# Attention with two expert layers on one core: the last tile pair closed tile by tile, the first two score tiles as whole float32 products, and 64-token products with both words side by side

## The chip, the cores and the metric

The kernel runs on one core of one Trainium2 chip. The metric is the device time of one execution in microseconds (us). Three runs of the kernel before gave 1182.36, 1183.76 and 1184.87 us; their median is 1183.76 us. Engines are named as in the profile: PE is TensorE's products (PEld its weight loads), DVE is VectorE, ACT is ScalarE, POOL is GpSimd, SP issues the DMAs.

## What is computed

```python
scores = q @ k.T / sqrt(64)                 # 4 batches x 8 heads, 576 x 576
mask   = scores >= (32nd largest of the row)
attn   = exp(where(mask, scores, -1e9) - rowmax)
attn   = attn / (attn.sum(-1) + 1e-9)
x      = attn @ v                           # 2304 tokens x 512
h      = relu(x @ w_in);  x = (h * h) @ w_out            # first expert layer, d_ff = 2048
h      = x @ w_in2;       out = max(0.01*h, h) @ w_out2  # second expert layer
```

All inputs are float32; the expert weights arrive as 64-bit words, of which the kernel builds float32 on the chip.

## The kernel before

**Precision.** A product is made of float32 words split in two: a high word that TensorE multiplies in one pass (type `fp32r`) and the low word that is left. `split_q` and `split_k` make the words of q and k: ACT or POOL copies the high word (`split_hi`, L129 and L131), DVE or POOL subtracts (L289, L272). q and k of a head come stored twice, in partitions 0 to 63 and 64 to 127; k keeps its high word in the first and its low word in the second, so that two products, with q's high and q's low word, give one score half. Products whose operands are typed plain float32 (`av`, L436, and the transposes L350, L365, L386) need no words.

**Attention.** The 2304 tokens are cut into units of 256, 64 or 320 tokens of a batch (`UNITS`). A unit and a pair of heads (`uh`) give tiles of 128 score rows, and two tiles are a pair of 16 slots on a time scale. For each tile `scores` makes two halves of 288 keys in PSUM and ACT copies them to `s` (L310, L311). The 32 largest of each row come from seven DVE instructions: four MAX8 (L932), each of eight values, and three MATCH_REPLACE8 between them (L934). Then `drop` (L329) and `expo_sum` (L333) on ACT make the exponentials, `recip` (L338 to L341) the reciprocal sums, `pt_main` (L350, L360) and `pt_left` (L365 to L401) the transposed probabilities `PT` and the row of reciprocals `rb`, `av` (L436) the product with v, and `x_out` (L467, L468, L472) the normed result and its two words xh and xl, the expert layers' input.

**The two stages.** The first block of the expert layers holds 512 tokens: units 0 and 1, which are pairs 0 to 15. The last of these pairs (`first_done`, 15) closes the block, and the expert layers start then, on PE; the attention of the other units runs on beside them, with probabilities in two words (`norm`, `av_split` L447, L452, L453). Unit 3 has 64 tokens: its `av_split` makes for each head eight products with 64 columns (four chunks of keys, high and low word) and one for the rest.

**Expert layers.** `moe` goes through 16 slices of d_ff. For each it makes h (L653), the activation and its two words ga, gh, gl (L663 to L673), and adds to acc (L690 in layer one, L692 in layer two). The weights of each slice are converted once from the raw words: ACT copies the low (L543) and high part (L552), DVE joins them (L559), ACT and POOL split them (L563, L564). The first two slices' weights are converted ahead, in `lead_passes` (L583, L584) and `lead_bits` (L590, L591, two DVE passes each: the shifted bits, then the sign).

**What sets the order.** The program lists its steps by slot (`at`), `urgent` raises a step's priority, `behind(key)` puts an instruction behind another of its engine. A scheduler then lays down a fixed order for each engine and for each DMA queue, and a pool's buffers can add waits. Each engine works through its order strictly.

## Time and profile before

| | |
|---|---|
| Runs, median (lowest to highest) | 1183.76 us (1182.36 to 1184.87) |
| Profiled execution, its own time | 1181.85 us |
| Its span, first to last instruction | 1180.1 us |
| Around the span | 1.75 us |
| Busy: PE, PEld, DVE, ACT, POOL | 1120.4, 984.7, 840.8, 817.0, 746.4 us |
| Mean granted TensorE clock | 0.989 of full speed |

The span falls in a stage before the expert layers, to 184.45 us, in which attention alone runs, and the rest, in which PE works almost without a break. A share of the whole span therefore says little; each stage has its own limit.

### The profile page before, as it was taken

The page shows a single profiled execution, that of the slowest core. Times are in us where ns is not written, and L with a number is a line of the kernel's source. Part 1 is how long each engine was busy: PE and PEld are TensorE (multiplying, and loading weights), DVE is VectorE, ACT ScalarE, POOL GpSimd, SP SyncE. Part 2 cuts the span into 40 slices and gives each one's busy share as a digit, 9 for nine tenths or more (in the row PEclk, how much of TensorE's full clock was granted, in tenths as well). Part 3 has the DMA queues.
Part 4 walks back from the last instruction along what each step waited for, and adds up shares of the span by engine and source line. Part 5 has one row for each costly group of instructions (what it writes and reads, how often), then busy time and mean ns, then how long its engine had stood idle before and what let it go on. Part 6 is the DMA issues. An engine that isn't in the chain of part 4 may idle for free.

```text
span 1180.1 us, 20025 instructions
## 1 busy us (share of the span) xinstructions
PE 1120.4 (95%) x6376; PEld 984.7 (83%) x6376; DVE 840.8 (71%) x1771; ACT 817.0 (69%) x1823; POOL 746.4 (63%) x960
## 2 busy tenths in 40 slices
PE   5898978899899999999999999999999999999998
PEld 4777766687678899989999998888788899999997
DVE  7999998867675669999999999989999200110011
ACT  6899997999889778877677677556866633333322
POOL 7968837899878767667898776767756543002100
PEclk9899988999999999999999999999999999999999
DMA  9768766999999588899988888667676489779974
GB/s 305 271 211 285 252 223 220 376 344 326 341 339 363 213 325 287 274 308 373 328 284 297 300 273 306 227 209 236 228 229 205 156 319 341 258 249 355 345 256 135
DMA packets 108201, 329.53 MB, mean 279 GB/s; under 512 B 17216, under 2 KB 25408, under 8 KB 104000
## 3 DMA queue, kind: packets, MB, share of 16 engines
q1 hardware_dynamic: 105472, 323.53, 79.3%
q10 hardware_dynamic: 2624, 4.72, 1.1%
q8 instruction: 52, 0.85, 0.3%
q14 instruction: 53, 0.43, 0.1%
HBM read 257.03 MB, written 71.17 MB: 278 GB/s over the span
## 4 chain that ended last, share of the span: by engine, by line
PE 70%; ACT 10%; DVE 7%; DMA 3%; issue 2%; POOL 2%; ACTq 0%; SPq 0%; POOLq 0%; DVEq 0%
PE h L653 28%; PE acc L692 15%; PE acc L690 13%; PE att L447 4%; DVE m L932 4%; PE att L350 3%; DVE w L934 3%; PE att L436 2%; ACT stage L311 1%; ACT e L333 1%; PE att L310 1%; PE sp L310 1%; ACT e L329 1%; ACT s L311 1%; DMA vraw<-in_v_dram 1%
## 5 line engine op out<-in xcount | busy, mean ns | idle before, releaser
L653 PE MATMUL h<-xh,wi 128*128 128x512 f32 (+2 forms) x1280 | 346.4, 343 | 8.8 <-ACT xh L704 3.5
L932 DVE MAX8 m<-w 128x8 f32<-128x576 f32 x432 | 311.1, 747 | 2.2
L653 PEld LDWEIGHTS h<-xh,wi 128*128 128x128 f32 x1280 | 226.1, 189 | 34.9 <-ACT ga L670 4.8
L673 POOL TENSOR_TENSOR gl<-ga,gh 128x512 fp32r<-128x512 f32 (+2 forms) x160 | 162.3, 1017 | 126.6 <-ACT gh L672 108.6
L934 DVE MATCH_REPLACE8 w<-m,w 128x576 f32<-128x576 f32 x288 | 213.0, 742 | 0.6
L653 PE MATMUL h<-xl,wi 128*128 128x512 f32 (+2 forms) x640 | 204.5, 339 | 0.0
L358 POOL TENSOR_TENSOR PTs<-whole,PTs 128x512 fp32r<-128x512 f32 x112 | 144.5, 1297 | 43.3 <-ACT whole L357 39.8
L690 PE MATMUL acc<-gh,wo 128*128 128x512 f32 (+2 forms) x768 | 157.0, 343 | 0.9 <-ACT gh L664 0.9
L692 PE MATMUL acc<-wo,gh 128*128 128x512 f32 x576 | 153.2, 397 | 0.2 <-ACT gh L672 0.2
L690 PEld LDWEIGHTS acc<-gh,wo 128*128 128x128 f32 x768 | 127.1, 190 | 13.1 <-ACT gh L664 1.7
L653 PEld LDWEIGHTS h<-xl,wi 128*128 128x128 f32 x640 | 120.3, 190 | 10.7
L329 ACT ACTIVATE e<-s,m 128x576 f32<-128x576 f32 x144 | 112.2, 782 | 24.1 <-DVE m L932 16.2
L932 DVE MAX8 m<-s 128x8 f32<-128x576 f32 x144 | 104.4, 748 | 30.3 <-ACT s L311 26.3
L673 DVE TENSOR_TENSOR gl<-ga,gh 128x384 fp32r<-128x384 f32 x32 | 17.9, 559 | 151.2 <-ACT gh L672 148.5
L670 ACT ACTIVATE ga<-h 128x512 f32<-128x512 f32 (+2 forms) x96 | 46.4, 489 | 114.1 <-PE h L653 112.1
L692 PEld LDWEIGHTS acc<-wo,gh 128*128 128x128 f32 x576 | 104.6, 188 | 20.0 <-ACT gh L672 0.4
L333 ACT ACTIVATE e<-e,nb 128x576 f32<-128x576 f32 x144 | 111.3, 778 | 4.8 <-POOL nb L323 4.7
L934 DVE MATCH_REPLACE8 w<-m,s 128x576 f32<-128x576 f32 x144 | 106.8, 743 | 0.3
L350 PE MATMUL att<-ident,e 128*128 128x128 f32 x576 | 88.5, 277 | 7.4 <-ACT e L333 6.7
L665 POOL TENSOR_TENSOR ga<-ga 128x512 f32<-128x512 f32 (+2 forms) x80 | 66.1, 828 | 44.0 <-ACT gh L664 41.6
L345 POOL TENSOR_SCALAR e<-e,rc 128x576 f32<-128x576 f32 x112 | 82.6, 748 | 11.5 <-DVE rc L341 10.9
L447 PE MATMUL att<-PTs,VT 128*128 128x256 f32 (+2 forms) x504 | 86.9, 297 | 2.0 <-ACT whole L357 1.7
(101 smaller groups left out, 2065.6 us busy)
## 6 DMA issues: line engine op xcount, KB each, us to landing
wi<-wd SPq DMA_DIRECT2D x160, 512.0 KB, 5.2
wo<-wd SPq DMA_DIRECT2D x160, 512.0 KB, 5.1
wraw<-in_w_dram SPq DMA_DIRECT2D x32, 1024.0 KB, 8.2
sd<-stage SPq DMA_DIRECT2D x76, 288.0 KB, 3.2
s<-sd SPq DMA_DIRECT2D x76, 288.0 KB, 5.0
wd<-wi SPq DMA_DIRECT2D x32, 512.0 KB, 7.4
wd<-wo SPq DMA_DIRECT2D x32, 512.0 KB, 7.3
vd<-VT SPq DMA_DIRECT2D x16, 640.0 KB, 6.3
```

The lines of the kernel that those rows point to most:

```text
L329: ACT.activation(t["e"], t["s"], AF.Prelu, bias=pr["m8"][:, i, 31:32], scale=-1.0, alpha=1.0 / FAR)
L333: ACT.activation(e, e, AF.Exp, bias=pr["nb"][:, i:i + 1], scale=-FAR, accum_out=pr["sum"][:, i:i + 1])
L345: POOL.tensor_scalar(e, e, pr["rc"][:, i:i + 1], 1.0, op0=OP.mult, op1=OP.mult)
L350: PE.transpose(ps[:, j * P:(j + 1) * P], t["e"][:, j * P:(j + 1) * P], ident)
L358: POOL.tensor_tensor(pts[:, 4:8, c:c + P], whole, pts.bitcast(F)[:, 0:4, c:c + P], op=OP.subtract)
L447: PE.matmul(ps, lhsT=l, rhs=r, start=i == 0, stop=i == len(mm) - 1)
L653: PE.matmul(two[r][:, 0:n], lhsT=ws[r][:, w, c * P:(c + 1) * P], rhs=x[c][y][:, 0:n], start=cnt == mine[0], stop=cnt == mine[-1])
L673: (DVE if j >= GLD else POOL).tensor_tensor(gl[:, 0:n], a[:, 0:n], gh.bitcast(F)[:, 0:n], op=OP.subtract)
L690: PE.matmul(acc[c][:, 0:n], lhsT=wo[:, w, cs], rhs=g[:, 0:n], start=first, stop=last)
L692: PE.matmul(acc[c], lhsT=g[:, cs], rhs=wo[:, w, :], start=first, stop=last)
L932: cur["dve"] = DVE.max(out=m8[:, x, 8 * r:8 * r + 8], in_=t["s"] if r == 0 else t["w"])
L934: cur["dve"] = DVE.match_replace(out=t["w"], in_to_replace=m8[:, x, 8 * r:8 * r + 8], in_values=t["s"] if r == 0 else t["w"], imm_value=NEG)
```

## The change

Five edits. (1) The first two score tiles (first head of the first unit) are one plain float32 product a half, straight from the raw q and k in 64 partitions (`kt` and the words are not used); q and k of that head pair are loaded in three pieces each, the first head's upper piece first, and their low words are made on POOL instead of DVE. (2) The last pair, 15, is closed tile by tile by `close`: the DVE does all seven instructions of tile 0 ahead of the last of tile 1, each tile has its own shift, sum, reciprocal, transposes and `rb`. Pair 14 is made urgent, its shift and sum go to DVE and ACT; pair 16's first MAX8 waits behind the shift. (3) The joining of the first two slices' weights takes one DVE pass instead of two, since ACT's copy of the high part (`Prelu` with a slope of 2^32) now carries the sign. (4) The third slice's first conversion waits behind the last xh (`closed`). (5) `av_split` of 64 tokens multiplies a chunk of v with both words side by side, 128 columns at once, and POOL adds the two halves.

```diff
-KLO_D = ((0, 0), (0, 1))
-QLO_D = (0,)
+KLO_D = ()
+QLO_D = ()
...
+        if st["i"] == 0:
+            SP.dma_start(st["k"][0:D, 0], k[b, hp, 0:D, 0])
+            cur["k"] = st["k"]
+            return
         SP.dma_start(st["k"], k[b, hp])
+
+    def load_k_rest(b, hp, st):
+        SP.dma_start(st["k"][D:P, 0], k[b, hp, D:P, 0])
+        SP.dma_start(st["k"][:, 1], k[b, hp, :, 1])
...
-        mm = [(x[:, h, c:c + P], kt[:, h, ks]) for h, c in t["parts"] for x in d]
+        mm = [(uh["q"][0:D, 0, t["i"] * P:t["i"] * P + P], cur["k"][0:D, 0, ks])] if t["i"] < 2 else [(x[:, h, c:c + P], kt[:, h, ks]) for h, c in t["parts"] for x in d]
...
+    def close(pr, i):
+        t, uh, m = pr["t"][i], pr["t"][i]["uh"], slice(i, i + 1)
+        if i == 0:
+            pr["nb"] = pool.tile([P, 2], F, tag="nb", name="nb", bufs=2)
+        cur["shift"] = DVE.tensor_tensor(pr["nb"][:, m], pr["m8"][:, i, 31:32], pr["m8"][:, i, 0:1], op=OP.subtract)
+        drop(pr, i)
+        expo_sum(pr, i)
+        ACT.activation(pr["sum"][:, m], pr["sum"][:, m], AF.Copy, bias=1e-9)
+        cur["recip"] = DVE.reciprocal(pr["rc"][:, m], pr["sum"][:, m])
+        pt_main(t)
+        ps = stage_psum.tile([P, 512], F, tag="sp", name="sp", bufs=SPB)
...
+        PE.transpose(ps[0:LEFT, 0:P], t["e"][:, NJ * P:S], ident)
+        ACT.activation(PT[0:64, 4, c:c + P], ps[0:64, 0:P], AF.Copy)
+        PE.transpose(ps[:, P:2 * P], pr["rc"][:, m].to_broadcast([P, P]), ident)
...
+        ACT.activation(uh["rb"][D:2 * D, r0:r0 + P], ps[D:2 * D, P:2 * P], AF.Copy)
...
+        if n == 64:
+            mm = [(vt[:, h, j, :], pts[:, j:j + 5:4, c]) for j in range(NJ)]
+        else:
+            mm = [(vt[:, h, j, :], pts[:, x + j, c]) for j in range(NJ) for x in (0, 4)]
...
+        if n == 64:
+            POOL.tensor_tensor(xf[mine, 0:n], xf[mine, 0:n], xf[mine, n:m], op=OP.add)
...
-            ACT.activation(b, raw[:, :, 0], AF.Copy, scale=L_SCALE, bias=L_BIAS)
+            with behind("closed") if i == 2 else ExitStack():
+                ACT.activation(b, raw[:, :, 0], AF.Copy, scale=L_SCALE, bias=L_BIAS)
...
-            ACT.activation(v, hi.bitcast(F), AF.Copy, scale=H_SCALE)
+            ACT.activation(v, hi.bitcast(F), AF.Prelu, scale=H_SCALE, alpha=2.0 ** 32)
...
-                DVE.scalar_tensor_tensor(b, vu, 0x80000000, b, op0=OP.bitwise_and, op1=OP.bitwise_or)
...
+                at(z + 6 + 7 * i, urgent(close), pr, i)
...
+            if p == first_done:
+                x, r, top = i // 7, i % 7 // 2, i % 7 % 2 == 0
+            t = pr["t"][x % 2]
+            if i < 14 and top:
+                with behind("shift") if p == first_done + 1 and r == 0 else ExitStack():
```

How the orders move, at three places.

**The start, SP and ACT.** SP's first DMAs and ACT's first copies; `_148` and `_151` are the first q and k, `_157` (now `_161`) and `_170` (now `_174`) the second and third q, `s0` and `s1` the first two tiles' scores. SP before, then SP in the change, then ACT in the change:

```order
L279 DMA qraw_148<-in_q_dram 128x2x256
L235 DMA kraw_151<-in_k_dram 128x1152
L279 DMA qraw_157<-in_q_dram 128x2x256
L279 DMA qraw_224<-in_q_dram 128x2x256
L279 DMA qraw_226<-in_q_dram 128x2x320
```

```order
L288 DMA qraw_148<-in_q_dram 64x256
L294 DMA qraw_148<-in_q_dram 64x256
L290 DMA qraw_161<-in_q_dram 128x2x256
L236 DMA kraw_151<-in_k_dram 64x576
L242 DMA kraw_151<-in_k_dram 64x576
L243 DMA kraw_151<-in_k_dram 128x576
L295 DMA qraw_148<-in_q_dram 128x256
```

```order
L129 ACTIVATE KT_150<-kraw_151 128x576
L327 ACTIVATE s0_101<-sd_176 128x288
L129 ACTIVATE KT_150<-kraw_151 128x576
L129 ACTIVATE q00_77<-qraw_148 128x256
L327 ACTIVATE s0_101<-sd_182 128x288
L327 ACTIVATE s1_102<-sd_185 128x288
L129 ACTIVATE q00_77<-qraw_174 128x256
L327 ACTIVATE s1_102<-sd_188 128x288
```

k's first piece is the fourth DMA, where all of k was the second; the second halves of s0 and s1 stand behind copies of pieces that land later.

**The last pair, DVE.** From the last MAX8 of pair 14 (`m8_2304`) on; `m8_2398` is pair 15, `m8_2506` (now `m8_2508`) pair 16, `xn_2414` the third head pair's result. Before, then in the change:

```order
L932 MAX m8_2304<-w_2308 128x8
L934 MATCH_REPLACE w_2401<-m8_2398,w_2401 128x576
L934 MATCH_REPLACE w_2402<-m8_2398,s1_102 128x576
L932 MAX m8_2398<-w_2401 128x8
L932 MAX m8_2398<-w_2402 128x8
L467 TENSOR_TENSOR xn_2414<-att_2390,rb_2267 128x256
...
L932 MAX m8_2506<-s2_103 128x8
L932 MAX m8_2398<-w_2402 128x8
L341 RECIPROCAL rc_2306<-sum_2305 128x2
```

```order
L979 MAX m8_2304<-w_2308 128x8
L509 TENSOR_TENSOR xn_2414<-att_2390,rb_2267 128x256
L979 MAX m8_2398<-w_2401 128x8
L339 TENSOR_TENSOR nb_2387<-m8_2304 128x2
...
L979 MAX m8_2398<-w_2402 128x8
L981 MATCH_REPLACE w_2402<-m8_2398,w_2402 128x576
L357 RECIPROCAL rc_2306<-sum_2305 128x2
L979 MAX m8_2398<-w_2402 128x8
L363 TENSOR_TENSOR nb_2442<-m8_2398 128x1
L636 SCALAR_TENSOR_TENSOR wc_2311<-v_2314,wc_2311 128x512
L979 MAX m8_2508<-s2_103 128x8
```

Pair 16's first MAX8 has left the place ahead of pair 15's last; xn has come to stand right behind pair 14's last MAX8, and pair 14's reciprocal ahead of pair 15's last.

**The first expert products, PE.** From the last h products of the first two slices on (`xl0` by `wi`), `h_2674` (now `h_2676`) being the third slice's h. Before, then in the change:

```order
L653 MATMUL h_2561<-xl0_672,wi_2351 128x512 x2
L310 MATMUL att_2570<-KT_2046,q01_83 128x288
L310 MATMUL att_2570<-KT_2046,q11_84 128x288
L310 MATMUL att_2598<-KT_2046,q01_83 128x288
L310 MATMUL att_2598<-KT_2046,q11_84 128x288
L690 MATMUL acc_2638<-gh_2615,wo_2313 128x512 x2
```

```order
L698 MATMUL h_2563<-xl0_672,wi_2351 128x512
...
L698 MATMUL h_2676<-xh0_671,wi_2567 128x512
L698 MATMUL h_2676<-xl0_672,wi_2567 128x512
...
L698 MATMUL h_2676<-xh0_671,wi_2567 128x512 x4
L326 MATMUL att_2685<-KT_2046,q01_83 128x288
L326 MATMUL att_2685<-KT_2046,q11_84 128x288
L735 MATMUL acc_2640<-gh_2617,wo_2313 128x512 x2
```

The twelve products of the third slice's h now stand ahead of the first acc products instead of behind them.

## Rows read from the trace of the kernel before

**Rows 1.** Stretches: us, busy of each engine (instructions), granted clock, DMA share, GB/s.

```profile
9.02:171.46 162.44, 139.83 (x798) 114.01 (x799) 159.28 (x344) 145.40 (x403) 122.32 (x183) 0.98 0.78 258
171.46:184.45 12.99, 10.56 (x42) 7.05 (x41) 12.43 (x28) 9.27 (x22) 7.74 (x10) 0.78 0.59 220
184.45:200.00 15.55, 11.66 (x47) 9.31 (x46) 12.52 (x26) 13.18 (x29) 9.40 (x12) 0.81 0.61 202
...
400.00:1000.00 600.00, 594.21 (x3635) 537.88 (x3634) 496.83 (x1076) 408.58 (x911) 414.74 (x540) 1.00 0.80 274
```

**Rows 2.** Timeline of the start: start, us, engine, line, operation [idle before <- what ended it].

```profile
1.45 0.58 SPq L235 DMA_DIRECT2D kraw<-in_k_dram  x1
...
5.63 1.26 ACT L129 ACTIVATE KT<-kraw 128x576 fp32r<-128x576 f32 x2 [0.90 <-DMA kraw<-in_k_dram]
...
9.02 0.76 DVE L932 MAX8 m<-s 128x8 f32<-128x576 f32 x1 [1.25 <-ACT s L311]
...
10.90 0.42 ACT L129 ACTIVATE q<-qraw 128x256 fp32r<-128x256 f32 x1 [0.38 <-DMA qraw<-in_q_dram]
```

**Rows 3.** Timeline, plain float32 products of av, near the seam and just ahead.

```profile
174.45 3.30 PE L436 MATMUL att<-PT,VN 128*128 128x256 f32 x8 [0.30 <-ACT PT L360]
...
181.37 2.62 PE L436 MATMUL att<-PT,VN 128*128 128x256 f32 x10 [1.09 <-ACT PT L360]
```

**Rows 4.** Timeline of DVE, PE and ACT around the last pair's end.

```profile
161.14 1.42 DVE L932 MAX8 m<-w 128x8 f32<-128x576 f32 x2
...
163.42 1.66 PE L436 MATMUL att<-PT,VN 128*128 128x256 f32 x6
...
165.25 0.41 DVE L467 TENSOR_TENSOR xn<-att,rb 128x256 f32<-128x256 f32 x1
...
170.04 0.76 DVE L932 MAX8 m<-s 128x8 f32<-128x576 f32 x1 [0.75 <-ACT s L311]
170.72 0.74 DVE L932 MAX8 m<-w 128x8 f32<-128x576 f32 x1
...
179.70 1.12 ACT L543 ACTIVATE wc<-wraw 128x1024 uint32<-128x1024 uint32 x1
...
184.45 1.32 PE L653 MATMUL h<-xh,wi 128*128 128x512 f32 x5
...
185.33 0.41 ACT L468 ACTIVATE xh<-xn 64x256 fp32r<-64x256 f32 x1
```

**Rows 5.** Groups of DVE instructions from 171.46 to 184.5 us: busy us, mean ns.

```profile
L591 DVE SCALAR_TENSOR_TENSOR wc<-v,wc 128x512 uint32<-128x512 uint32 x4 | 2.6, 676 | 0.0
```

**Rows 6.** Timeline of PE and POOL behind the first expert products.

```profile
189.83 1.09 PE L653 MATMUL h<-xl,wi 128*128 128x512 f32 x4
...
194.84 0.85 PE L310 MATMUL att<-KT,q 128*128 128x288 f32 x2 [3.66 <-ACT s L311]
195.92 0.79 PE L690 MATMUL acc<-gh,wo 128*128 128x512 f32 x1 [0.23 <-ACT gh L664]
...
199.18 1.29 POOL L564 TENSOR_TENSOR wi<-wc,wi 128x512 fp32r<-128x512 f32 x1
```

**Rows 7.** Timeline of PE, av_split products with 256 and with 64 columns.

```profile
399.39 0.99 PE L447 MATMUL att<-PTs,VT 128*128 128x256 f32 x7
400.22 0.39 PE L653 MATMUL h<-xh,wi 128*128 128x512 f32 x1
...
414.79 1.08 PE L447 MATMUL att<-PTs,VT 128*128 128x64 f32 x9
415.71 0.48 PE L692 MATMUL acc<-wo,gl 128*128 128x512 f32 x1
```

**Rows 8.** The chain that ended last, a piece at 415 us: start, us, piece.

```profile
414.95 0.92 PE att L447 x9
```

**Rows 9.** Stretch 558 to 640 us, and the chain's shares in it.

```profile
558.00:640.00 82.00, 79.75 (x504) 78.09 (x504) 81.22 (x177) 60.26 (x131) 71.10 (x93) 1.00 0.88 302
by line: DVE m L932 48.2%; DVE w L934 37.3%; DVE PTs L375 4.1%; DVE xf L453 3.2%; issue 3.1%; ACT e L333 1.1%; ACT e L329 1.0%; ACT PTs L355 0.7%; DVE xl L705 0.7%; ACT whole L357 0.6%; DVE rc L341 0.5%; ACT tmp L452 0.5%; DVEq L932 0.0%
```

82 lines of the change are left out of this document (46 added, 36 removed).

## The prediction

> **What bounds the kernel now.** I read the stretches first, then the timeline at the two places where the limit changes (the start and the seam, by which I mean the time from the last pair's last MAX8 to the expert layers' first acc products), then the chain that ended last where the edit on the 64-token products lies.
>
> From the first MAX8 to the last one of pair 15 the DVE is busy 159.28 of 162.44 us [rows 1]: this stage is DVE's, and ACT with 145.40 is not far behind. In the seam no engine is full: PE has 10.56 of 12.99 us and then 11.66 of 15.55, at a granted clock of 0.78 and 0.81 [rows 1] (means over time at both levels), and what ends its waits are results of ACT. From 400 to 1000 us PE is busy 594.21 of 600 us [rows 1]: there a microsecond of PE work taken away is a microsecond of the span, as long as nothing else takes the limit. So a gain at the start counts if the DVE keeps it, a gain in the seam counts if PE's first expert products really come sooner, and a gain in the 64-token products counts on PE.
>
> The profiled execution took 1181.85 us; the median of the runs is 1.91 us above. I sum against the first and add 1.91.
>
> **The start.** The first MAX8 begins at 9.02 [rows 2]. All of k is the second DMA, its issue begins at 1.45, and ACT waits for it until 5.63 [rows 2]; then come two copies by ACT, two corrections by DVE, four products and two copies to s, in all 3.39 us. In the change the first tiles wait only for k's first piece and q's. Two bounds for its landing: it is the fourth DMA instead of the second, at 0.58 us an issue [rows 2] 1.2 us later; or the bytes decide, 528 KB up to its end instead of 832 (256 of q and 576 of k), and at the 258 GB/s of the stage [rows 1] that is 1.2 us sooner. I take 0.5 sooner, since ACT's wait for k shows the load itself to be the limit: 5.1. A plain float32 instruction of 256 columns takes 0.41 us at TensorE's lower level (1.2 GHz, 3.30 by 8) and 0.26 at or near its upper one (2.4 GHz, 2.62 by 10) [rows 3]; I take the lower for the start, where PE has done nothing yet. A score half needs two of 288 columns, so 0.93 (an estimate from those rows), and the two halves 1.9. With 0.42 for the copy, the scores could be there at 7.4. But ACT's order puts the second k copy (1.26 by 2 = 0.63 [rows 2]) and a q copy (0.42) ahead of the second half's copy, and what they wait for lands last: about 6.8 + 0.63 + 0.42 + 0.42 = 8.3. Gain 0.7 us. Against it: tile 1's second half stands behind the copy of the third q, which today lands for a copy at 10.90 [rows 2]; that would make tile 1 complete at 11.7, where the DVE wants it three instructions after 8.3, at 10.4. I keep **0.5 us of gain**; ends 1.2 of gain and 0.7 of loss. The two corrections that leave the DVE (nothing else could run there) and reach POOL cost nothing beyond that as long as POOL stays ahead of tile 2.
>
> Against the loads speaks the Trainium skill, "SBUF — State Buffer", "Door 1": 64 partitions reach only half of the 16 ports, 196 against 328 GB/s. By that the k piece of 144 KB lands 0.3 us later (an estimate from that page), the start gains 0.2 and the time becomes 1178.6; no row here shows a load to 64 partitions in this place.
>
> **The seam.** Five parts.
> (a) DVE up to pair 15's last MAX8: pair 16's MAX8 leaves (0.68 from start to start) with its wait of 0.75 [rows 4], and three small instructions of about 0.15 come ahead: -1.0.
> (b) ACT's conversion of the third slice, 1.12 us at 179.70 [rows 4], stood between the two copies of the last transposes; it now waits behind the last xh: -1.1.
> (c) xn of the third head pair moves from behind five larger instructions to right behind pair 14's last MAX8. That MAX8 ends at 162.56, the av product that xn needs ended at 165.08 [rows 4]: a new wait between 0 and 2.5 us, and behind it stand all of pair 15's remaining instructions. I take +1.5, nearer to the row, since PE's work ahead of that product is much the same.
> (d) Closing by tile lets tile 0's drop, exponentials and transposes run while the DVE finishes tile 1. ACT has no fewer instructions by it, and it is ACT's order that carries the chain; I count 0, with 1.6 of gain (two ACT passes of 0.8) as the end. The four DVE passes of weight bits that go, 0.676 us each [rows 5], lie off this chain, which waits for ACT; their 2.6 us are counted at 0 too.
> (e) Behind the first h products PE idles 3.66 and 0.23 us ahead of acc [rows 6]. The order now has the twelve products of the third slice's h there; at 0.23 us each (four in 1.09, one alone 0.39 [rows 6, 7]) that is 2.8 us of work done in the gap. ACT has the third slice's conversion ahead of its ga now, which takes back half: -1.4.
> Sum of the seam **-2.0 us**; with all at their better ends -6.4 (c at 0, d at -1.5, e at -2.8).
>
> **The 64-token products.** Nine products of 64 columns take 0.92 us from first start to the next group's start (414.79 to 415.71), 0.102 each; seven of 256 columns take 0.83, 0.118 each [rows 7]. So the width hardly matters here, and the weight load sets the pace. The change leaves five of the nine: four of 128 columns and one of 64. Price between 0.102 and 0.118: saved 4 x 0.102 = 0.41, or 0.92 - 4 x 0.118 - 0.10 = 0.35; by eight products (four head pairs, two heads) 3.3 or 2.8. The far end on the other side: if a product between 64 and 256 columns were charged like plain float32, 0.26 us for 256 columns and two instructions [rows 3], so 0.26 for 128: 4 x 0.26 + 0.10 = 1.14, a loss of 0.22 by eight, 1.8. I take **-3.0**, nearest to the rows of the same operand type. The chain runs through these products, 0.92 us of PE at 414.95 and more of the kind [rows 8]. POOL's eight adds, ACT's and DVE's wider copies are some tenths each, beside PE work; if they were not hidden, the next xh would be later, which PE reads only at the next block.
>
> The Trainium skill, "TensorE: Matmul & The Clock Gate", "Back-to-back issue gap", gives a product of 128 columns 56 ns alone: by that the weight load stays the limit, the saving is 3.3 and the time 1178.0. No row shows a product of that type with 128 columns.
>
> **Sum.** -0.5 - 2.0 - 3.0 = -5.5: 1176.35 in place of 1181.85, and on the scale of the median **1178.3 us**.
>
> **Rivals.**
> 1. *The wide products cost like float32.* +1.8 in place of -3.0: 1183.76 - 2.5 + 1.8 = 1183.1. For it: no row between 64 and 256 columns. Against: 64 and 256 cost nearly the same. Chance 0.15.
> 2. *The DVE takes the limit later.* Between 558 and 640 us the chain runs on the DVE, 48.2% and 37.3% for its two top-32 instructions, and it is busy 81.22 of 82 us [rows 9]. What PE gained at 415 us alone would be waited away there; start and seam bring the DVE forward too and stay: -2.5, 1181.3. Against: PE is busy 79.75 of the 82 us itself. Chance 0.13.
> 3. *Slower: the third slice's weights come too late.* Their conversion began at 179.70 and now waits for the last xh, which ended at 185.74 [rows 4]. Today the low word of wi ends at 200.47 [rows 6], 20.8 us after the conversion began; PE could let that wait, because acc stood ahead. Now the third h stands ahead of acc. At the old lag it would start at 185.74 + 20.8 = 206.5 and acc after it, against 195.92: 10.6 us lost in place of part (e). Total -0.5 - 0.6 - 3.0 + 10.6 = +6.5: 1190.3. It decides from a lag of 14.3 us. Against it: those 20.8 us are mostly queueing behind work that was urgent in the seam; the passes alone are ACT 1.12, two DVE passes of 0.68, and POOL 1.29 [rows 4 to 6]. Chance 0.11.
> 4. *More: the seam at its better ends.* -0.5 - 6.4 - 3.0 = -9.9: 1173.9. For it: PE idles in the seam and runs at 0.8 of its clock [rows 1], and fewer gaps would mend both. Chance 0.12.
> That the early start is lost to tile 1's wait (the first edit does not do what it says) would cost 1.2 against my sum, 1179.5; it lies within the forecast.
>
> **How the numbers follow.** The forecast has the rest, 0.49. Measurements of this kernel tell about 0.2%, 2.4 us, from no change: faster means below 1181.4. The forecast and rival 4 lie there, and half of rival 2, which sits on the edge: 0.66. Rival 1 and the other half of rival 2 with a little of the forecast: 0.23. Rival 3: 0.11. The range reaches from rival 4 to just past rival 1, 1173.5 to 1184.0, which leaves out rival 3 and a little at the low end.
>
> **What would show it.** First MAX8 near 8.3 us, and no idle DVE at its fourth instruction. Pair 15's last MAX8 near 171; a DVE wait at xn of 1 to 2 us. First expert products near 183.5, the twelve products of the third h ahead of acc without a wait over 1 us. Five products of 64 tokens in about 0.55 us, 32 fewer in all: the count falls from 72 to 40. I am wrong if those five take over 0.9 us, if PE waits for the third slice's wi, or if PE's idle time grows between 558 and 640 us by what it lost before.

## The result and the profile after

The changed kernel took **1195.89 us** (median of 6 runs, 1192.39 to 1198.84), against 1183.80 for the kernel before in the same rounds: a ratio of 1.0104, with a 95% interval of 1.0084 to 1.0124. It is 12 us slower; the forecast was 5.5 us faster, and its range ended at 1184.0. The profiled execution took 1192.98 us with a span of 1191.2; by engine PE was busy for 1124.9 us, DVE 839.9, ACT 816.9, POOL 754.0, at a mean granted clock of 0.983.

Two stretches of the changed kernel that answer to [rows 1], from the profile's windows (us, then busy time and instructions of PE, PEld, DVE, ACT and POOL, granted clock, DMA share, GB/s):

```profile
9.02:171.46 162.44, 135.55 (x745) 109.71 (x745) 150.06 (x321) 136.12 (x378) 117.58 (x176) 0.95 0.75 245
...
400.00:1000.00 600.00, 592.18 (x3586) 532.78 (x3585) 503.01 (x1085) 410.83 (x912) 422.14 (x550) 1.00 0.80 271
```

In the first stretch the DVE, whose stage this is, does 150.06 us of work in place of 159.28. To see where the stage now ends I cut both kernels at their own marks: the first MAX8, the last shift (the subtraction that the DVE does behind pair 15's last MAX8) and the first h product. Before, then changed:

```profile
9.02:172.16 163.14, 140.53 (x800) 114.39 (x800) 159.98 (x345) 146.10 (x404) 122.32 (x183) 0.97 0.78 259
172.16:184.45 12.29, 9.86 (x39) 6.67 (x39) 11.73 (x25) 8.57 (x21) 7.74 (x10) 0.80 0.56 207
```

```profile
9.21:182.67 173.46, 144.53 (x797) 116.92 (x796) 161.01 (x345) 144.79 (x401) 124.34 (x184) 0.95 0.73 240
182.67:197.78 15.11, 11.73 (x47) 8.20 (x47) 12.78 (x26) 10.74 (x30) 8.80 (x10) 0.77 0.84 298
```

The first h product comes 13.33 us later (197.78 against 184.45). Of these, 0.19 lie ahead of the first MAX8, **10.32 between the first MAX8 and the last shift** (173.46 against 163.14; I call this the long piece), and 2.82 between the last shift and the first h (15.11 against 12.29). Behind it 2.2 us come back: the span is 11.1 us longer. In the long piece the DVE's work is nearly the same, 345 instructions in both and 161.01 us against 159.98; it is **idle for 12.45 us instead of 3.16**.

The last shift is a handy mark but not quite the same place in both. In the kernel before, a reciprocal and an instruction of pair 16 stand between pair 15's last MAX8, which ends at 171.46 [rows 4], and the shift; in the changed kernel the shift follows the MAX8 directly (its row, the last of the next fence, ends at 182.63). From the end of that MAX8 the first h comes 12.99 us later before and 15.15 us in the change: the closing then costs 2.2 us, and the long piece 11.0.

Where the DVE idles, the changed kernel's timeline shows, at the start and between 75 and 118 us:

```profile
6.06 4.49 PE L326 MATMUL sd<-kraw,qraw 64*128 64x288 f32 x8 [6.06 <-DMA kraw<-in_k_dram]
...
9.21 0.76 DVE L979 MAX8 m<-s 128x8 f32<-128x576 f32 x1 [9.21 <-ACT s L327]
...
13.23 0.42 ACT L129 ACTIVATE q<-qraw 128x256 fp32r<-128x256 f32 x1 [3.41 <-DMA qraw<-in_q_dram]
...
13.98 0.76 DVE L979 MAX8 m<-s 128x8 f32<-128x576 f32 x1 [2.36 <-ACT s L327]
...
181.89 0.74 DVE L979 MAX8 m<-w 128x8 f32<-128x576 f32 x1
```

```profile
75.68 13.52 SPq L330 DMA_DIRECT2D sd<-stage  x7
...
101.13 0.71 ACT L327 ACTIVATE stage<-sp 128x288 f32<-128x288 f32 x2 [3.95 <-DMA sd<-stage]
...
101.59 1.63 PE L326 MATMUL sp<-KTa,q 128*128 128x288 f32 x5 [3.90 <-ACT stage L327]
...
112.84 0.17 DVE L357 RECIPROCAL rc<-sum 128x2 f32<-128x2 f32 x1 [2.11 <-POOL sum L356]
...
117.56 0.76 DVE L979 MAX8 m<-s 128x8 f32<-128x576 f32 x1 [3.17 <-ACT s L327]
```

The wait of 2.36 us at 13.98 is the one that the prediction spoke of: tile 1's second half stands behind the copy of the third q, which lands for 13.23 now, 2.3 us later than in [rows 2]. The other place was not foreseen. Scores made ahead go to DRAM through five buffers (`stage`). SP issues seven of these stores in a row, each behind ACT's copy, 13.52 us long, and what stands behind them in SP's order bunches afterwards. ACT then waits 3.95 us for a store to give a buffer back, PE waits for ACT, and scores and sums come late for the DVE. Over 75 to 118 us the DVE idles 6.94 us, in the kernel before 0.97. That its waits of 2.11 and 3.17 us follow from the one for the store is read from their places, not shown. The same stretch by pieces, from the changed kernel's windows (columns as above), shows what follows for PE:

```profile
98.00:100.00 2.00, 0.00 (x0) 0.00 (x0) 0.85 (x2) 0.00 (x0) 1.92 (x3) 0.76 0.99 372
100.00:102.00 2.00, 0.41 (x1) 0.40 (x2) 1.79 (x4) 0.87 (x3) 2.00 (x5) 0.50 0.79 303
102.00:104.00 2.00, 2.00 (x10) 1.98 (x10) 2.00 (x5) 2.00 (x6) 2.00 (x4) 0.50 0.77 236
...
106.00:108.00 2.00, 2.00 (x12) 1.60 (x10) 2.00 (x6) 1.68 (x5) 2.00 (x2) 1.00 0.91 340
```

PE does nothing from 98 to 100, and from 100 to 104 it works at a granted clock of 0.50 (1.2 GHz).

### The profile page after: what moved, and what is told of

It is laid out like the page before. It is cut to its first block, busy times and chain, and to the rows that moved or that the text cites. A ratio compares the mean times of both kernels' runs of the same rounds, so it can differ in the third digit from the quotient of the medians.

```text
span 1191.2 us, 19987 instructions
## 1 busy us (share of the span) xinstructions
PE 1124.9 (94%) x6344; PEld 986.4 (83%) x6344; DVE 839.9 (71%) x1766; ACT 816.9 (69%) x1827; POOL 754.0 (63%) x970
## 4 chain that ended last, share of the span: by engine, by line
PE 57%; ACT 2%; DMA 2%; DVE 2%; issue 0%; ACTq 0%; POOL 0%; POOLq 0%
PE h L698 25%; PE acc L737 13%; PE acc L735 12%; PE att L486 4%; PE att L385 3%; PE att L326 1%; DVE m L979 1%; PE att L400 1%; DMA wi<-wd 1%; DVE w L981 1%; DMA s<-sd 1%; DMA wo<-wd 1%; ACT PTs L390 0%; ACT whole L392 0%; ACT e L349 0%
## 5 line engine op out<-in xcount | busy, mean ns | idle before, releaser
L735 PEld LDWEIGHTS acc<-gh,wo 128*128 128x128 f32 x768 | 126.9, 190 | 11.7
L735 PE MATMUL acc<-gl,wo 128*128 128x512 f32 (+2 forms) x384 | 87.9, 349 | 0.3 <-POOL gl L718 0.3
```

The lines of the kernel that those rows point to most:

```text
L735: PE.matmul(acc[c][:, 0:n], lhsT=wo[:, w, cs], rhs=g[:, 0:n], start=first, stop=last)
```

## The experiments

I asked first which edit makes the long piece (theory A: the start; theory B: the closing of the last pair), then by what (A1: the loads in pieces; A2: any edit at the head makes the scheduler lay out every order behind it anew, and that order loses), then what the closing by tile costs. The numbering of edits is that of the change. "Last shift" and "first h" are as above, each from the run's one profile, and one profile scatters. Kernels that have the same orders on every engine at these places show how much: e8 and e2, the same up to about 400 us, differ by 1.2 us at the last shift, by 2.9 at the first h and so by 1.7 in the piece between; the changed kernel and e4 differ by 2.9 at the last shift, the kernel before and e3 by 1.3. Smaller differences between two runs are not told from scatter below. `FILL`, used from the ninth run on, is the range of slots over which the scores made ahead are spread; moving its end from 222 to 224 leaves every instruction as it is and changes only orders, from about 75 us on, while (8, 224) changes them from the start.

| run | what it has | median us | ratio [95%] | last shift | first h | between |
|---|---|---|---|---|---|---|
| before | none of the edits | 1183.80 | 1 | 172.16 | 184.45 | 12.29 |
| after | all five | 1195.89 | 1.0104 [1.0084, 1.0124] | 182.67 | 197.78 | 15.11 |
| e1 | edit 1 | 1201.18 | 1.0156 [1.0118, 1.0193] | 181.79 | 192.59 | 10.80 |
| e2 | edits 2 to 5 | 1188.12 | 1.0050 [1.0034, 1.0067] | 169.40 | 183.25 | 13.85 |
| e3 | edit 5 | 1181.60 | 0.9994 [0.9975, 1.0012] | 170.83 | 183.25 | 12.42 |
| e4 | all but 4 | 1202.59 | 1.0158 [1.0128, 1.0188] | 179.79 | 195.35 | 15.56 |
| e5 | edit 1, loads whole | 1187.87 | 1.0035 [1.0016, 1.0054] | 174.82 | 186.52 | 11.70 |
| e6 | loads in pieces only | 1200.08 | 1.0133 [1.0106, 1.0160] | 179.50 | 188.72 | 9.22 |
| e7 | low words on POOL only | 1194.89 | 1.0089 [1.0062, 1.0117] | 177.97 | 187.61 | 9.64 |
| e8 | edits 2 to 4 | 1182.35 | 0.9977 [0.9963, 0.9991] | 170.60 | 186.18 | 15.58 |
| e9 | none, FILL (2, 224) | **1175.79** | 0.9941 [0.9923, 0.9959] | 170.36 | 181.09 | 10.73 |
| e10 | all, FILL (2, 224) | 1187.92 | 1.0043 [1.0025, 1.0060] | 181.81 | 196.05 | 14.24 |
| e11 | all but 5 | 1195.09 | 1.0103 [1.0076, 1.0130] | 181.51 | 196.63 | 15.12 |
| e12 | edits 2 and 3 | 1183.81 | 1.0009 [0.9994, 1.0024] | 171.53 | 186.13 | 14.60 |
| e13 | all, FILL (8, 224) | 1192.94 | 1.0070 [1.0043, 1.0097] | 176.55 | 192.60 | 16.05 |
| e14 | none, FILL (8, 224) | 1183.31 | 1.0001 [0.9987, 1.0015] | 177.44 | 186.85 | 9.41 |
| e15 | edits 2 to 4, FILL (2, 224) | 1185.54 | 1.0025 [1.0010, 1.0041] | 169.64 | 183.53 | 13.89 |
| e16 | edit 5, FILL (2, 224) | 1176.11 | 0.9936 [0.9919, 0.9953] | 171.18 | 180.57 | 9.39 |
| e17 | e8, av placed later | 1182.59 | 0.9987 [0.9970, 1.0003] | 171.14 | 185.01 | 13.87 |
| e18 | e17, FILL (2, 224) | 1180.47 | 0.9967 [0.9950, 0.9984] | 170.25 | 184.34 | 14.09 |

**e1, edit 1 alone.** The kernel before with the first edit of the change:

```diff
-KLO_D = ((0, 0), (0, 1))
-QLO_D = (0,)
+KLO_D = ()
+QLO_D = ()
...
+            SP.dma_start(st["k"][0:D, 0], k[b, hp, 0:D, 0])
...
+            SP.dma_start(t[0:D, 0, 0:n], q[0, 0, 0:D, 0, 0:n])
...
+        mm = [(uh["q"][0:D, 0, t["i"] * P:t["i"] * P + P], cur["k"][0:D, 0, ks])] if t["i"] < 2 else [(x[:, h, c:c + P], kt[:, h, ks]) for h, c in t["parts"] for x in d]
```

> The kernel before with the first edit alone (first two tiles' scores as whole float32, the loads in pieces, the low words on POOL). Theory A, the first edit makes the loss of the first stage: the order of every engine up to about 160 us is then the changed kernel's, so the DVE's idle time up to its 127th MAX8 and its delay there (7.2 us in the changed kernel) come back, and the time is 7 to 10 us above before, about 1192. Theory B, the loss is made at the seam by closing tile by tile: this kernel keeps only the wait of tile 1 (2.4 us) and lies at 1184 to 1187.

**e2, the change without edit 1.** The same lines the other way round:

```diff
-KLO_D = ()
-QLO_D = ()
+KLO_D = ((0, 0), (0, 1))
+QLO_D = (0,)
...
-            SP.dma_start(st["k"][0:D, 0], k[b, hp, 0:D, 0])
...
-            SP.dma_start(t[0:D, 0, 0:n], q[0, 0, 0:D, 0, 0:n])
```

> The changed kernel without its first edit: the other four stay. Theory A: the first stage is that of before, its last MAX8 of the last pair near 171 us, and the seam and products edits show their own worth, 1179 to 1183. Theory B: the seam stays as long as in the changed kernel (15.2 us from the last MAX8 to the first expert product) with PE at its lower level, 1188 to 1193.

The last shift comes at 181.79 with the first edit alone and at 169.40 without it: A holds for the long piece, B falls there. But e2 is still slower than before, though its first h is 1.2 us sooner. It loses behind 460 us, in waits such as these (windows of e2, columns as above):

```profile
640.00:645.00 5.00, 3.31 (x13) 2.51 (x13) 4.93 (x11) 2.76 (x9) 1.62 (x4) 0.65 0.48 164
```

PE has 3.3 of 5 us while the DVE is full. Neither e8 (edits 2 to 4, with e2's orders up to about 400 us) nor e3 (edit 5), both below, ends with such a loss; it belongs to neither alone.

**e3, the products alone.**

```diff
-        mm = [(vt[:, h, j, :], pts[:, x + j, c]) for j in range(NJ) for x in (0, 4)]
+            mm = [(vt[:, h, j, :], pts[:, j:j + 5:4, c]) for j in range(NJ)]
...
+            POOL.tensor_tensor(xf[mine, 0:n], xf[mine, 0:n], xf[mine, n:m], op=OP.add)
```

> The kernel before with the wide 64-token products alone. As forecast: five products in about 0.55 us in place of nine in 0.92, eight times, 3.0 us less PE time at 400 to 460 us and about 1181. Rival, the other engines set the end at this place (POOL's added instruction, DVE at 450 to 640 us): the products are as cheap but PE's idle time grows by as much, within 1 us of before. Rival, wide products cost like float32: 1.8 us more.

The price is as forecast: the changed kernel's timeline has four products of 128 columns in 0.56 us, and the groups of instructions (busy us, mean ns) go from one row before to two after:

```profile
425.02 0.56 PE L486 MATMUL att<-PTs,VT 128*128 128x128 f32 x4
```

```profile
L447 PE MATMUL att<-PTs,VT 128*128 128x64 f32 x72 | 8.9, 265 | 0.0
```

```profile
L486 PE MATMUL att<-PTs,VT 128*128 128x128 f32 x32 | 4.5, 274 | 0.0
...
L486 PE MATMUL att<-PTs,VT 128*128 128x64 f32 x8 | 1.8, 226 | 0.0
```

That is 8.9 against 6.3, 2.6 us less. The time is the same all the same: 0.9994, where the forecast's 3.0 us would be 0.9975, the end of the interval. Up to 700 us, before and then e3 (windows):

```profile
400.00:700.00 300.00, 296.01 (x1980) 280.42 (x1979) 281.74 (x611) 223.87 (x517) 228.61 (x311) 1.00 0.86 302
450.00:700.00 250.00, 246.01 (x1607) 232.91 (x1607) 247.59 (x538) 189.34 (x429) 193.16 (x260) 1.00 0.87 303
```

```profile
400.00:700.00 300.00, 293.50 (x1945) 276.47 (x1945) 283.24 (x611) 223.55 (x518) 231.63 (x320) 1.00 0.86 302
450.00:700.00 250.00, 244.76 (x1589) 230.69 (x1588) 247.67 (x537) 187.03 (x427) 192.48 (x259) 1.00 0.86 303
```

PE's work over 400 to 700 us falls by 2.51 us and its idle time grows by as much, 3.99 to 6.50. Busy and idle time fill a window in any case; that e3 is no further on at its end the counts show, with 35 PE instructions fewer, of which the edit took 32, and 611 of the DVE in both. The DVE is busy for 247.6 of 250 us in both. What PE saves it waits away, beside a full DVE.

**e4, the change without the hold** (edit 4), tests whether that wait costs:

```diff
-            with behind("closed") if i == 2 else ExitStack():
-                ACT.activation(b, raw[:, :, 0], AF.Copy, scale=L_SCALE, bias=L_BIAS)
+            ACT.activation(b, raw[:, :, 0], AF.Copy, scale=L_SCALE, bias=L_BIAS)
```

> The changed kernel without the fourth edit, so that the third slice's first conversion may run ahead of the last xh. If the hold cost time (PE waits 2.31 us for the third slice's h ahead of acc), the first acc product comes 2 us sooner after the first h than the 11.9 us of the changed kernel and the time falls by 2 to 3 us, to about 1193. If the hold helped as forecast (1.1 us of ACT taken off the chain), the first h comes 1.1 us later against the last MAX8 and the time rises by as much, to about 1197. By theory A neither touches the first stage, whose delay of 7 us stays.

Slower still than the changed kernel, 1202.59, with the same 15 us behind the last shift: the hold is not what costs. The orders are the changed kernel's up to the hold, so the last shift 2.9 us sooner is scatter, and what e4 loses on the changed kernel comes behind the first h, which is 2.4 us sooner.

**e5, e6, e7, parts of edit 1 on the kernel before.** e5 has the float32 scores, made urgent as in edit 1, and POOL's low words, but whole loads; e6 has the loads in pieces alone (scores as before); e7 the two tables of low words alone. Their diffs:

```diff
+KLO_D = ()
+QLO_D = ()
...
+        if st["i"] == 0:
+            cur["k"] = st["k"]
         SP.dma_start(st["k"], k[b, hp])
...
+        mm = [(uh["q"][0:D, 0, t["i"] * P:t["i"] * P + P], cur["k"][0:D, 0, ks])] if t["i"] < 2 else [(x[:, h, c:c + P], kt[:, h, ks]) for h, c in t["parts"] for x in d]
```

```diff
+            SP.dma_start(st["k"][0:D, 0], k[b, hp, 0:D, 0])
...
+        SP.dma_start(st["k"][D:P, 0], k[b, hp, D:P, 0])
+        SP.dma_start(st["k"][:, 1], k[b, hp, :, 1])
...
+            SP.dma_start(t[0:D, 0, 0:n], q[0, 0, 0:D, 0, 0:n])
...
+        SP.dma_start(uh["q"][D:P, 0, 0:n], q[0, 0, D:P, 0, 0:n])
+        SP.dma_start(uh["q"][:, 1, 0:n], q[0, 0, :, 1, 0:n])
```

```diff
-KLO_D = ((0, 0), (0, 1))
-QLO_D = (0,)
+KLO_D = ()
+QLO_D = ()
```

> The kernel before with the float32 scores and the low words on POOL, but q and k loaded whole as before. Theory A1, the loss of the first edit comes from the loads in pieces (the third q lands late, tile 1 waits, and SP's order behind it makes ACT wait 3.9 us for a staged transfer at 97 us): no DVE wait at its fourth instruction, no wait of over 1.5 us near 97 us, and 1182 to 1185. Theory A2, any change at the head makes the scheduler lay the whole stage out anew, and it is that order that loses: a wait of ACT for staged transfers comes back somewhere between 60 and 130 us, and the time is 4 us or more above before.

> The kernel before with the loads of the first q and k in pieces, and nothing else: the scores are made from the words as before. Theory A1: this has the loss, 4 us or more above before, with a DVE wait behind the first three instructions and the ACT wait near 97 us. Theory A2: it loses too, but by a wait at a place of its own. If neither, the time is within 2 us of before.

> The kernel before with the low words of the first q and k made on POOL instead of DVE, and nothing else. POOL takes 1.4 us for a k correction, one half after the other, so the first MAX8 comes 1 to 2 us later. Theory A1: that is all, 1185. Theory A2: the order of the stage changes too, and the time is 4 us or more above before.

All three lose, 4, 16 and 11 us, so A1 is not the answer by itself. Of this the first h shows 2.1, 4.3 and 3.2 us; most of what e6 and e7 lose comes behind it. In e5 the early start works: PE has k at 5.66 and the first MAX8 is the second row below, 0.62 us sooner than in [rows 2], where the change's came 0.19 later. (The eleven kernels with the old start have it at 8.92 to 9.48, the six with the whole of edit 1 at 8.94 to 9.73.)

```profile
5.66 4.38 PE L312 MATMUL sd<-kraw,qraw 64*128 64x288 f32 x8 [5.66 <-DMA kraw<-in_k_dram]
...
8.40 0.76 DVE L936 MAX8 m<-s 128x8 f32<-128x576 f32 x1 [8.40 <-ACT s L313]
```

Yet its last shift is 2.7 us late. From first MAX8 to last shift the DVE has 160.28, 162.68 and 161.76 us of work in the three (before: 159.98) and idles 6.14, 6.49 and 6.47 (before: 3.16). None has the stall near 98 us. Nor do the parts add: e7's tables, 11 us alone, are also in e5, which loses 4. That fits A2, which e9 and e10 then tried without any edit at the head.

**e8, the closing alone** (edits 2 to 4); of its diff the core:

```diff
-            at(z + 13, urgent(shifts), pr)
...
+                at(z + 6 + 7 * i, urgent(close), pr, i)
```

> The kernel before with the second, third and fourth edits: closing by tile, one pass for the weights' bits, the hold on the third slice; no start edit, no wide products. The changed kernel without the start edit had its first expert product 1.2 us sooner and was 3 to 4 us ahead at 230 and 480 us, but lost 9 us between 480 and 650 us, where the DVE is 98% busy and PE waits in small pieces, each followed by a stretch at the lower clock. If that loss belongs to the seam edits' order (or to the DVE's limit), it is here too and the time is 3 to 6 us above before. If it belongs to the wide products beside them, it is gone here and the time is 1180 to 1182.

Faster than before by 2.7 us (1.1 to 4.4), about the seam's forecast of 2.0, but not in the way that the prediction had; that the size agrees is luck, as e12 and e15 below show. The last shift is 1.56 us sooner, 0.89 by the end of the last MAX8 (first row), and the piece behind it 3.29 us longer. Rows of its timeline show where:

```profile
169.81 0.76 DVE L952 MAX8 m<-w 128x8 f32<-128x576 f32 x1
...
174.77 4.77 PE L455 MATMUL att<-PT,VN 128*128 128x256 f32 x10
...
180.41 0.60 ACT L379 ACTIVATE PT<-att 128x512 f32<-128x512 f32 x1 [4.12 <-PE att L369]
...
204.37 1.22 PE L712 MATMUL acc<-gl,wo 128*128 128x512 f32 x2 [3.87 <-POOL gl L695]
```

Ten av products stand ahead of all but one of the last pair's transposes and take 4.77 us; ACT waits 4.12 for a transpose. Behind the first acc products PE waits 3.87 us. The kernel before has these ten av products ahead of its last transposes too, from 174.45 [rows 3], with the transposes behind them:

```profile
178.57 1.29 PE L350 MATMUL att<-ident,e 128*128 128x128 f32 x8
```

But there they begin 2.99 us behind the end of the last MAX8 and the transposes go on 7.1 behind it; in e8 it is 4.20 and 8.9. Edit 2 had moved this av on the time scale, from slot 27 to 23, and made it urgent.

**e9, e10, orders alone.** One number, on the kernel before (e9) and on the changed one (e10):

```diff
-FILL = (2, 222)
+FILL = (2, 224)
```

> The kernel before with one number changed: the staged scores of the later units are spread over slots 2 to 224 instead of 2 to 222. Every instruction and its size stay; only the orders that the scheduler lays down change, from about 75 us on. Theory A2 (what was lost is the order that fitted this chip, not the work of the edits): the time moves clear of before, most likely slower by 3 to 12 us. Rival theory D (the orders don't matter, the added instructions, waits and transfers do): within 2 us of before.

> The changed kernel with the same one number changed. Theory A2: the time moves by more than 3 us from the changed kernel's 1196, either way, since its order is one draw among others; the wait of ACT for staged transfers near 97 us (3.9 us) is another size. Theory D: 1194 to 1197, with the same waits.

Each kernel gets 7 to 8 us faster from another order of the same instructions, and e9 is the fastest of the study (with e16). That orders do not matter falls. The distance between the two kernels stays 12 us, though; their first 75 us kept their orders, and ACT's longest wait for a store near 98 us is still 3.7 us in e10. In e9 the third slice's h stands ahead of acc as well, though it has none of the edits.

**e11, the change without edit 5, and e12, the closing without the hold.** Edits as in e3 and e4, taken back.

> The changed kernel without the wide 64-token products. The first stage and the seam have the changed kernel's order. If each edit had a worth of its own that adds up, this would be the start edit's 18 us and the seam's -2.7 together, about 1199, 3 us above the changed kernel's, as forecast for the products. By theory A2 the edits don't add up: the order behind 390 us is drawn anew, and the time lies anywhere from 1190 to 1202.

> The kernel before with closing by tile and the single pass for the weights' bits, without the hold on the third slice's conversion. The hold was forecast to take 1.1 us off the chain to the first expert product and to let the third slice's h fill PE's wait ahead of acc. If so, the first h comes 1 us later against the last MAX8 than with the hold (15.6 us there) and the time is 1 to 3 us above that kernel, 1183 to 1185. Rival: the hold only moves the wait (PE waited 3.9 us for POOL's gl behind the first acc products with it), and the time is within 1 us of that kernel's 1182.

e11 is as slow as the change: the products neither cost nor give. e12 is level with before, and the time from last shift to first h is 14.60 without the hold and, with it, 15.58 in e8 and 13.85 in e2, which have the same orders there: a gain of the forecast's size, 1.1 us, is not told from the scatter, though e8 is a little faster as a whole. e12 shows something else, the wait at xn that the prediction's (c) spoke of:

```profile
166.58 0.42 DVE L486 TENSOR_TENSOR xn<-att,rb 128x256 f32<-128x256 f32 x1 [1.11 <-PE att L455]
```

**e13, e14, an order that is new from the start**, for the changed kernel and, as its control, the one before:

```diff
-FILL = (2, 222)
+FILL = (8, 224)
```

> The changed kernel with the staged scores spread over slots 8 to 224 instead of 2 to 222, so that the orders are new from the first microseconds on, those of ACT's and SP's staging among them; every instruction and its size stay. Theory A2 (the stage up to 170 us lost by the order of ACT and SP, not by the start edit's own work): ACT's wait for staged transfers near 97 us (3.9 us) and the DVE's 5 to 6 us of idle time at 110 to 118 us go, the DVE's delay at its 127th MAX8 is under 4 us, and the time is 1180 to 1187. Theory E (the start edit's own work makes it): the delay stays at 8 us or more and the time is above 1190.

> The kernel before with the same two numbers, the control for the run beside it: the difference between the two is what the five edits are worth at this order. Theory A2: the time is another draw, 1176 to 1190, and the difference is not the 12 us found at the two other orders. Theory E: the changed kernel is 10 to 14 us slower here too.

The long piece in e13, then in e14, from the first MAX8 to the end of pair 15's last one (windows):

```profile
9.12:176.51 167.39, 143.25 (x799) 115.85 (x798) 160.12 (x343) 145.49 (x404) 124.15 (x184) 0.97 0.75 252
```

```profile
9.02:175.05 166.03, 144.94 (x810) 118.05 (x811) 161.81 (x347) 148.65 (x410) 122.98 (x185) 0.96 0.77 262
```

The last shift would mislead here. In e14 an xn stands ahead of it in the DVE's order, and that waits 2.05 us; by the shift e13 would seem 0.9 us ahead of its control, by the last MAX8 it is 1.5 to 2.1 us behind (either of the two MAX8 in the row below can be pair 15's). e14's rows, then the longest wait of the DVE in e13:

```profile
173.65 1.40 DVE L932 MAX8 m<-w 128x8 f32<-128x576 f32 x2
177.10 0.42 DVE L467 TENSOR_TENSOR xn<-att,rb 64x256 f32<-64x256 f32 x1 [2.05 <-ACT rb L401]
```

```profile
155.80 0.76 DVE L979 MAX8 m<-s 128x8 f32<-128x576 f32 x1 [4.50 <-ACT s L327]
```

ACT's waits for a store between 60 and 130 us (us in total, times, longest) in the changed kernel, then in e13:

```profile
ACT stage L327 <- DMA sd<-stage: 4.5, 2, 4.0
```

```profile
ACT stage L327 <- DMA sd<-stage: 0.7, 1, 0.7
```

With every edit in it, e13 ends its last MAX8 1.5 to 2.1 us behind its control, within the scatter of same orders, where the changed kernel was 11.2 us behind the kernel before. **Most of the long piece was the order, not the work of edit 1**, as far as one other order can show it. That order has a wait of its own, the 4.50 us above; the DVE idles 7.27 us in e13 and 4.22 in e14 (the windows' lengths less its busy time). The totals in ACT's waits for a store go with it: 3.7 to 4.6 us in the five kernels that have the whole of edit 1 with `FILL` beginning at 2 (after, e1, e4, e10, e11), 0.2 to 1.7, or no such wait listed, in all others. e5, e6 and e7 lose without it, so it is one way to lose and not the only one.

But e13 was expected at 1180 to 1187 and took 1192.94. Its last MAX8 is also 5.1 us behind that of the kernel before, between A2's "under 4" and E's "8 us or more". Its first h comes 5.75 us behind its control's, 16.1 us behind the last MAX8 against 11.8 to 12.5. Even so PE has done as many h products by 240 us in both, e13 and then e14 (windows of the tile h; busy time of PE, PEld and ACT):

```profile
180.00:240.00 60.00, 21.13 (x84) 15.30 (x84) 3.99 (x7) 0.89 0.80 288
```

```profile
180.00:240.00 60.00, 23.05 (x84) 16.32 (x84) 3.69 (x7) 0.89 0.83 298
```

Counted through the two traces, the 150th of the h and acc products starts at 239.99 us in both, the 400th at 323.94 in e13 and 316.39 in e14. At this order the 8 to 10 us are thus lost behind 240 us; the later first h had been made good by then. Which edit loses them there is not shown. With three orders the changed kernel was slower than its control three times, by 10 to 12 us; chance of the draw is one reading, that the edits make every order worse is not excluded.

**e15, e16, the closing and the products at e9's order** (`FILL` (2, 224)):

> Closing by tile, one pass for the weights' bits and the hold, on the reordered kernel that took 1175.8 us (slots 2 to 224). If the seam edits have the worth that they showed alone (1.7 to 2.7 us), 1173 to 1175, the fastest of all. If that gain was a draw of the order as well, the time lies anywhere from 1172 to 1186.

> The wide 64-token products alone on the reordered kernel that took 1175.8 us. The order up to 390 us is the same. If the products' saving on PE is real and only hidden by an unlucky order, 1172.5 to 1174. If the wait moves to other engines behind 420 us whatever the order, within 1 us of 1175.8 or slower.

At that order the closing loses against e9 (1.0025 against 0.9941), the products are level with it (0.9936, within about 3 us). So the closing's small gain in e8 is no property of the edit.

**e17, e18, the av products behind the last transposes,** on e8 and e15:

```diff
-            z = 16 * (uh["lastA"] // 2 if hs == (0,) else uh["last"] // 2) + (15 if near else 23 if tight and apart else 30)
+            z = 16 * (uh["lastA"] // 2 if hs == (0,) else uh["last"] // 2) + (15 if near else 29 if tight and apart else 30)
...
-                at(z + i, urgent(av) if tight else av, uh, hs, i)
+                at(z + i, urgent(av) if near else av, uh, hs, i)
```

> Closing by tile with one pass and the hold, but the first half of the last head pair's av (ten plain float32 products) laid behind the last pair's transposes on PE instead of ahead of them. In every kernel that closes by tile these ten took 4.0 to 4.8 us at TensorE's lower level, ACT waited 3.3 to 4.1 us for the transposes behind them, and the last shift was 13.9 to 16.1 us ahead of the first expert product, against 9.2 to 12.4 us in the kernels that close by pair. Theory F (the lost seam is this order on PE): ACT's wait falls below 2 us and the distance from the last shift to the first h to 13 us or less; the time is 1 to 3 us below the same kernel with av ahead (1182.4 beside before's 1184.1), unless the order behind 200 us is a worse draw. Rival theory G (ACT has more instructions by the smaller pieces, or the clock alone makes it): the distance stays at 14 us or more.

> The same at the order with slots 2 to 224, where closing by tile took 1185.5 us and the kernel that closes by pair 1175.8. Theory F: the distance from the last shift to the first h falls from 13.9 us to 12 or less and the time below 1184. Theory G: it stays. If the time comes to 1174 to 1176, closing by tile is worth nothing at this order; below that it would be the fastest of all.

Two rows of e17's timeline, then one of e9's:

```profile
177.13 3.28 PE L455 MATMUL att<-PT,VN 128*128 128x256 f32 x10
...
180.70 0.27 ACT L360 ACTIVATE rb<-sp 64x128 f32<-64x128 f32 x1 [2.64 <-PE sp L357]
```

```profile
169.06 3.52 PE L436 MATMUL att<-PT,VN 128*128 128x256 f32 x8 [0.51 <-ACT PT L360]
```

In e17 ACT's wait falls from 4.12 to 2.64 us, but it is another wait: the transposes of the probabilities come ahead of av now, that of the reciprocals (L357), for which ACT waits, still stands behind ten av products. The piece falls from 15.58 to 13.87 where 13 or less was expected, and e2, with av ahead, had 13.85; so nothing is shown by it, and the time does not move. In e18 the piece stays (13.89 to 14.09), yet the time falls from 1.0025 to 0.9967, about 7 us: what e18 gains on e15 it gains behind the first h, and it remains slower than e9. In e9 such av products run at 169.06, ahead of the last shift at 170.36, where PE has room; with closing by tile they ran at 177.13 or 174.77, in the chain, and before at 174.45. Whether this makes the longer piece is not shown, and no run separates what the lower clock costs there.

## Why the prediction was wrong

**The start, forecast -0.5.** Two steps failed. The landing of k's first piece was put at 5.1; PE waited for it until 6.06 (5.84 to 6.07 in the six kernels with the whole of edit 1). In e5, where k came whole as the second DMA, PE began at 5.66: the pieces brought nothing forward. The Trainium skill ("SBUF — State Buffer", "Door 1") speaks against a load to 64 partitions, and an estimate from it put the landing at 5.4; the trace is later than both, in that direction, but no run loads the piece alone. With whole loads (e5) the start gained 0.62. The price of 0.41 for a plain float32 instruction was also low: it was read where the granted clock was 0.57 (174.45 to 177.59), and at 0.50 it is 0.48 (the last section). And tile 1 was put at 11.7 at worst, 0.7 us of loss; it came at 13.98, after 2.36 us of DVE idling.

**The start again: "cost nothing beyond that as long as POOL stays ahead of tile 2".** This is the step that lost the forecast. It priced the moved instructions where they stood and took the orders behind them as given; the part on the change compared orders at three places, and none lay between 20 and 160 us. In e6 and e7, where a load is only split or an instruction only changes its engine, the time is 16 and 11 us longer, 4.3 and 3.2 of it up to the first h. In the changed kernel 10.32 us went there, 9.29 of it DVE idle time, to waits that no row of before could show; at e13's order, with the same edits, the last MAX8 is level with its control's within the scatter. Why one order has such waits and another has not stays open, and so does why the changed kernel was slower at all three orders.

**The seam, forecast -2.0.** (a) cannot be told: -0.89 in e8 for -1.0, by the end of the last MAX8, but e3, with none of these edits and the orders of before, has -1.32. Nor can (b), with 14.60 us without the hold and 13.85 or 15.58 with it. (c), a wait of 1.5 us, came in e12 and e17 with 1.11 and 1.13 us, ended by the av product as forecast; in the changed kernel xn is done directly behind the MAX8, as in e2 and e8. (By the orders in the part on the change it had stood behind four larger instructions, not five.) (d) was counted at 0 with an end of -1.6. From the end of the last MAX8 to the first h all 11 kernels that close by tile take 13.9 to 16.1 us and all nine others 9.2 to 13.1; from the last shift it is 13.85 to 16.05 against 9.22 to 12.42. The first step in this is right: ACT's last exponentials end 4.91 us behind the last MAX8 before (176.37) and 4.84 in e8 (175.41), so ACT's own passes gain nothing. The step that failed is "it is ACT's order that carries the chain": the difference lies behind the exponentials, where the first h follows them after 8.08 us before and 10.77 in e8 (over all kernels, 5.5 to 8.2 by pair and 8.7 to 11.1 by tile), with ACT waiting for PE, 1.92 us before and 4.12 in e8. The changed kernel's timeline:

```profile
174.66 0.43 DVE L509 TENSOR_TENSOR xn<-att,rb 128x256 f32<-128x256 f32 x1
...
186.44 4.77 PE L471 MATMUL att<-PT,VN 128*128 128x256 f32 x10
...
191.73 0.60 ACT L395 ACTIVATE PT<-att 128x512 f32<-128x512 f32 x1 [2.75 <-PE att L385]
...
197.78 2.06 PE L698 MATMUL h<-xh,wi 128*128 128x512 f32 x8
...
206.60 0.50 PE L698 MATMUL h<-xh,wi 128*128 128x512 f32 x1 [2.31 <-ACT ga L708]
...
209.71 2.02 PE L735 MATMUL acc<-gh,wo 128*128 128x512 f32 x8
216.00 0.85 PE L326 MATMUL att<-KT,q 128*128 128x288 f32 x2 [4.27 <-DVE wc L604]
```

The ten av products take 4.77 us, 0.48 each, and ACT waits 2.75 us behind them. (e) was right in its place: the twelve products do run ahead of acc, which comes 11.93 us after the first h instead of 11.47 [rows 4, 6] with 2.8 us more work in between. With that work counted, the first acc comes as long after the last MAX8 as before (27.08 less 2.8 against 24.46). But PE waits 2.31 us there, and 4.27 us behind the first acc until the DVE has joined weights: the gain became a wait. How much of the loss lasts is open; by the 100th of the h and acc products, counted from the last MAX8, the kernels by tile (43.7 to 53.4 us) and by pair (39.7 to 49.7) overlap.

**The products, forecast -3.0.** The price was right, 2.6 us less work; what failed is "there a microsecond of PE work taken away is a microsecond of the span". The condition that followed it, "as long as nothing else takes the limit", did not hold: what rival 2 described came true for this edit, and over 450 to 700 us, not only 558 to 640.

**The rivals.** Rival 1 is false. Rival 2's way holds in e3, and the time of e16 agrees. Rival 3's sign came true by another way. In the changed kernel the third slice's low words are ready at 206.11 (the row below), 6.3 us behind the last xh (which ended at 199.80) and not 20.8, and the wait of 2.31 us was ended by ACT's ga. None of the rivals named what decided, a new order far from the edits.

```profile
204.84 1.27 POOL L609 TENSOR_TENSOR wi<-wc,wi 128x512 fp32r<-128x512 f32 x1 [2.69 <-ACT wi L608]
```

## What to carry to other kernels

Where a scheduler lays out the orders, an edit at the head of the program is an edit of everything behind it: compare whole orders, not the places edited, and measure against a control in which one harmless number draws another order, since here such draws moved the time by up to 8 us while the edits were forecast at 0.5 to 3. A saving on the engine that looks full counts only if the engine that is full next, here the DVE over 450 to 700 us, is relieved too. Closing work in smaller pieces did not shorten what follows it in any of 11 kernels here; look at what the other engines have in their orders behind it. And before two profiles are compared mark by mark, find out how far two profiles of the same order lie apart, here up to 2.9 us, and put the mark at the instruction that ends the work, not at one that may stand behind something else.

## What the runs showed of the hardware

In the changed kernel PE had no instruction from 97.70 to 101.59 us, the wait of 3.90 us above; the granted clock was 0.50 over 100 to 104 us and 1.00 again over 106 to 108. Plain float32 products of 256 columns took 0.48 us each in the seam, at a granted clock of 0.50 (the row below), and 0.26 in the second of [rows 3], where the granted clock was 1.00. A product of 128 columns of the word type costs little more than one of 64: 0.14 us of busy time (4.5 by 32) against 0.12 (8.9 by 72).

```profile
186.44:191.14 4.70, 4.70 (x11) 2.86 (x10) 4.63 (x10) 2.51 (x8) 2.58 (x4) 0.50 0.94 321
```
